# Windowed attention, Mish layer and experts on one core: the activation's intermediate moves into the low part's buffer, and two more weight pieces are converted during attention

## The chip, the cores and the metric

The kernel runs on one core of a Trainium2 chip. The metric is the device time of one execution in microseconds; the median of several executions counts. The program keeps five engines: TensorE (PE, matmuls; its weight loads are listed as PEld), VectorE (DVE), ScalarE (ACT), GpSimd (POOL) and SyncE (SP), which issues all DMA transfers here.

## The reference

What has to be computed, cut to the lines that matter (B 2, H 8, S 768, D 64; 1536 tokens, model width 512):

```python
# windowed attention: 4 sink columns and a window of 128
scores = np.where(keep, scale * q @ k.T, -1e9)
a = softmax(scores)
x = (a @ v)                                   # [1536, 512]
# Mish layer, weights in float64, d_ff 2048
h = x @ w_in
g = h * np.tanh(np.log1p(np.exp(np.minimum(h, 20.0))))
x = g @ w_out
# four experts of width 1024, weighted by domain probabilities
out += p[:, e:e + 1] * (np.maximum(x @ w1[e], 0.0) @ w2[e])
```

## The kernel before

All dense products are made from three fp32r matmuls: every operand is kept as a high part and a low part, and high times high, low times high and high times low are summed in PSUM (`TERMS`, L366). Activations have their parts in `xh` and `xl`; a layer's hidden tiles have theirs in `gh` and `gl`.

The dense work is cut into units of 512 hidden columns (`Experts.units`, L394). Units 0 to 3 are the Mish layer, units 4 to 11 the experts. A unit has its weights in four SBUF tiles, `wih`, `wil`, `woh` and `wol`; units take turns between two pools, `m_w0` and `m_w1` (L390, L597). A unit goes over the tokens in chunks. For each chunk `layer1` (L465) makes four hidden tiles: 12 matmuls into a PSUM tile `h` (L477), then the activation, which ends in `gh` and `gl`. `layer2` (L491) makes from these four output tiles `o` of 12 matmuls each (L504). `stream` (L449) writes the layer-1 steps of a chunk in between the layer-2 steps of the chunk before. Unit 0 has four chunks, called A, B, C and D here: tokens 0 to 255, 256 to 511, 512 to 1023 and 1024 to 1535. The four hidden tiles of chunk C are called C0 to C3 below; in the build of the kernel before they bear the names `h_1537`, `h_1636`, `h_1790` and `h_1941`.

The Mish activation (`mish`, L541) is a chain over two engines: four ACT operations from `h` to an exponential `r` (L549 to L552), one DVE operation (L553), one on ACT (L554), two on DVE (L555, L556; L556 is the last that reads `h`), one on ACT that writes `gh` and one on POOL that writes `gl` (L557, by way of L89 and L97).

While attention runs, the PSUM is shared with it: `x.psum(first, 1, 1)` (L575) gives unit 0 one bank for `h` (`m_pa`) and one for `o`, and `r` lies in an SBUF pool `m_pr` of one buffer. Chunks A and B and the tiles C0 to C3 use this one `h` bank. When attention has been written out, `first.close()` (L596) gives back its pools, `m_w1` takes their SBUF room, and new PSUM pools with three `h`, three `o` and two `r` banks are opened (L598); chunk D and all later work use these.

The Mish weights come as float64. `split_double` (L100) turns a piece of 128 x 1024 words into its two parts: one ACT operation (L116), seven on DVE (L117, L118, L119, L121, L122, L123, L124) and a DMA of the high part (L120). Units 0 and 1 and the first half of unit 2 are converted in the attention loop (L584 to L595): four pieces of unit 0 with the items 0 to 3, and six more, for unit 1 and for `wi` of unit 2, with the items named in `PARK`. These six are parked in DRAM by DMA (L120, L126) and loaded later by plain DMA (L434). The other pieces, `wo` of unit 2 and all of unit 3, are converted when their turn comes (L438).

The order of each engine's queue is not the order of the source: the framework's scheduler sorts the instructions of all engines when the program is built, and what comes out is fixed. Each engine then takes its queue in that order and waits at an instruction whose inputs or buffer are not ready.

Of the kernel before, what the change touches and what calls it, by code (L numbers as in the profile page):

```python
# [9 lines left out]
F32 = mybir.dt.float32  # L10
# [3 lines left out]
AF = mybir.ActivationFunctionType  # L14
ALU = mybir.AluOpType
PSUM = bass.MemoryType.PSUM

P = 128
BIG = 8.0e9
C2, C1, C0 = 0.4889076793633006, -0.9463237919407588, -0.8989585617169157  # L20
# [7 lines left out]
AHEAD = 2  # L28
LAG = 5
WARM = 12  # L30
PARK = (8, 10, 12, 14, 16, 18)

class Ctx:
    pass
# [42 lines left out]
def normalize_probs(c):  # L77
    nc = c.nc
    nc.vector.tensor_reduce(c.ps, c.pn, axis=mybir.AxisListType.X, op=ALU.add)
    nc.vector.tensor_scalar(c.ps, c.ps, 1e-9, None, ALU.add)  # L80
    nc.vector.reciprocal(c.ps, c.ps)
    nc.vector.tensor_tensor(c.pn, c.pn, c.ps.to_broadcast([P, 12, 4]), ALU.mult)
# [11 lines left out]
def split(c, hi, lo, src, eng_hi, eng_lo):  # L94

    copy(c, eng_hi, hi, src)
    eng_lo.tensor_tensor(lo, src, hi.bitcast(F32), ALU.subtract)  # L97
# [31 lines left out]
def load_item(c, b, hp, i, pool=None):  # L129

    w = c.KW[min(i, 1)]
    raw = c.stage.next() if pool is None else pool.tile([P, QW + c.KW[1]], F32, tag="qk", name="qk")
    off = c.OFF[i]
    c.nc.sync.dma_start(out=raw[:, 0:QW + w], in_=c.qk[b, hp, :, off:off + QW + w])
    return raw
# [29 lines left out]
def banded_masks(c):  # L165

    nc = c.nc
    rel, sink, diag, prev = c.parts
    m0, m1, m2 = c.masks
    nc.vector.tensor_scalar(sink, sink, c.ns, None, ALU.is_ge)  # L170
    nc.vector.scalar_tensor_tensor(diag, rel, c.win, diag, ALU.is_ge, ALU.add)
    nc.vector.scalar_tensor_tensor(m0[:, 0:P], diag, -BIG, sink, ALU.mult, ALU.mult)
    nc.vector.tensor_scalar(prev, rel, float(P), c.win, ALU.add, ALU.is_ge)
    nc.vector.scalar_tensor_tensor(m1[:, 0:P], prev, -BIG, sink, ALU.mult, ALU.mult)
    for m, at, x in ((m1, P, diag), (m2, 0, prev), (m2, P, sink[:, 0:SINKS]), (m2, SEG, diag)):
        nc.gpsimd.tensor_scalar(m[:, at:at + x.shape[1]], x, -BIG, 0.0, ALU.mult, ALU.add)
# [11 lines left out]
def attention_pools(c, ctx):  # L188
    nc = c.nc
    a = Ctx()  # L190
    a.qk = ctx.enter_context(c.tc.tile_pool(name="a_qk", bufs=4))
    v = c.acc[:, 8:12].rearrange("p a w -> p (a w)")
    a.v = Ring([v[:, 3 * P * n:3 * P * (n + 1)].rearrange("p (n d) -> p n d", n=3) for n in range(5)])
    a.p = ctx.enter_context(c.tc.tile_pool(name="a_p", bufs=3))
    a.st = v[0:4 * SINKS, 15 * P:16 * P]
    a.sm = ctx.enter_context(c.tc.tile_pool(name="a_sm", bufs=3))
    a.ps = ctx.enter_context(c.tc.tile_pool(name="a_ps", bufs=3, space=PSUM))
    a.tr = ctx.enter_context(c.tc.tile_pool(name="a_tr", bufs=2, space=PSUM))
    a.pv = ctx.enter_context(c.tc.tile_pool(name="a_pv", bufs=1, space=PSUM))
    a.vsk = c.vsk  # L200
    return a


def attention_values(c, a, b, hp, i):

    v = a.v.next()
    n0 = 0 if i else 1
    c.nc.sync.dma_start(
        out=v[:, n0:3],
        in_=c.v[b, hp, (2 * i - 1 + n0) * P:(2 * i + 2) * P, :].rearrange("(n p) d -> p n d", p=P),  # L210
    )
    return v
# [165 lines left out]
class Experts:  # L378
# [26 lines left out]

    def psum(self, ctx, nh, no, nr=0):
        tp = self.c.tc.tile_pool
        self.pr = ctx.enter_context(tp(name="m_pr", bufs=nr or 1, **(dict(space=PSUM) if nr else {})))
        self.pa = ctx.enter_context(tp(name="m_pa", bufs=nh, space=PSUM))
        self.pb = ctx.enter_context(tp(name="m_pb", bufs=no, space=PSUM))  # L410

# [129 lines left out]
    def mish(self, n, gh, gl, h):  # L541

        c, nc = self.c, self.c.nc
        cw = h.shape[-1]
        w, u = (self.tp.tile([P, self.CW], F32, tag=t, name=t)[:, 0:cw] for t in ("w", "u"))
        r = self.pr.tile([P, self.CW], F32, tag="r", name="r")[:, 0:cw]
        nc.scalar.activation(w, h, AF.Tanh, scale=0.5)  # L549
        nc.scalar.activation(w, w, AF.Square, scale=-0.5, bias=0.5)  # L550
        nc.scalar.activation(u, w, AF.Square, scale=C2, bias=C1)
        nc.scalar.activation(r, u, AF.Exp, bias=C0)  # L552
        nc.vector.scalar_tensor_tensor(u, w, 1.0, r, ALU.add, ALU.mult)  # L553
        nc.scalar.activation(u, u, AF.Square, scale=ROOT2, bias=-1.5 * ROOT2)  # L554
        nc.vector.scalar_tensor_tensor(u, u, 1.5, r, ALU.add, ALU.mult)  # L555
        nc.vector.scalar_tensor_tensor(w, u, 1.0, h, ALU.subtract, ALU.mult)  # L556
        split(c, gh, gl, w, nc.scalar, nc.gpsimd)  # L557


def run(gen, n=None):  # L560

    while n is None or n > 0:
        if next(gen, run) is run:
            return
        n = None if n is None else n - 1


def banded(c, ctx, raws):

    tc = c.tc  # L570
    banded_masks(c)
    first = ExitStack()
    x = Experts(c, ctx)
    w = x.weights(0)
    x.psum(first, 1, 1)  # L575
    a = attention_pools(c, first)
    steps = x.stream([(0, 0, QW), (0, QW, QW)] + [(0, t0, x.CW) for t0 in range(2 * QW, c.T, x.CW)] + later(c, x, 1))
    dram = ctx.enter_context(tc.tile_pool(name="park", bufs=1, space=bass.MemoryType.DRAM))
    w = chain(w, x.park(dram, 1, "wi"), x.park(dram, 1, "wo"), x.park(dram, 2, "wi"))
    items = c.items  # L580
    raws = dict(enumerate(raws))
    preps = {}
    done = 0
    for m, it in enumerate(items):  # L584
        while done <= min(m + AHEAD, len(items) - 1):
            raw = raws.pop(done) if done in raws else load_item(c, *items[done], pool=a.qk)
            preps[done] = raw, attention_values(c, a, *items[done])
            done += 1
        attention_item(c, a, *it, preps.pop(m))
        if m < 4 or m in PARK:  # L590
            run(w, 1)
        if m >= LAG:
            run(steps, 1)
        if m == 0:
            normalize_probs(c)  # L595
    first.close()  # L596
    x.wpool[1] = ctx.enter_context(tc.tile_pool(name="m_w1", bufs=1))  # L597
    x.psum(ctx, 3, 3, 2)  # L598
    run(x.weights(1))
    run(steps, 4 * (x.NF + 4) - 4 - (len(items) - LAG))  # L600
    rest(c, x, steps, 1)


def later(c, x, first):

    return [(n, t0, x.CW) for n in range(first, len(x.units)) for t0 in range(0, c.T, x.CW)]


def rest(c, x, steps, first):

    per = (c.T // x.CW) * (x.NF + 4)
    for n in range(first, len(x.units)):
        w = x.weights(n + 1) if n + 1 < len(x.units) else iter(())
        for _ in range(per // 2):
            run(steps, 2)
            run(w, 1)
        run(w)
    run(steps)
# [15 lines left out]
def swa_mish_experts_kernel(ctx: ExitStack, tc: tile.TileContext, qk, v, vsink, n_sink, window, w_in, w_out, probs, w1,  # L634
# [35 lines left out]
    with tc.If(flag > 0) as cmp:  # L670
        with ExitStack() as s:
            banded(c, s, raws)
# [69 lines left out]
```

## Time and profile before

| | us |
|---|---|
| median of 3 runs | 936.74 |
| lowest and highest of them | 935.36 and 939.33 |
| the profiled execution | 931.33 |
| its span, first to last instruction | 929.5 |
| PE busy in the span | 905.6 |
| DVE busy | 424.6 |
| ACT busy | 347.7 |
| POOL busy | 263.7 |

The span is what the trace covers; 1.8 us of the profiled execution lie outside it. Matmuls overlap in the array, so a busy PE isn't a PE at its best rate: at full clock 12 matmuls of 512 columns take 2.72 us from start to start, though one alone is shown with 0.39 us. A row of the timeline has start, duration, engine, line, operation, output and inputs, and in brackets the engine's idle time ahead of it with what ended it.

### The profile page before, as it was taken

What the parts mean: (1) busy time and instruction counts of PE and PEld (TensorE: products, weight loads), DVE (VectorE), ACT (ScalarE), POOL (GpSimd) and SP (SyncE); (2) the same over time, 40 slices, a digit from 0 to 9 for tenths busy, and PEclk for the clock granted to TensorE, in tenths of its full rate; (3) what the DMA queues carried; (4) which work ended last, traced back from release to release, by engine and by line L of the source; (5) the groups of instructions that cost most, each with busy time, mean ns of one, the idle gap of its engine ahead of it and who ended that gap; (6) DMA issues with size and microseconds to landing.
All of it is one profiled execution on the core that took longest, in us unless ns stands there. A gap on an engine that the chain in (4) does not pass through costs nothing.

```text
span 929.5 us, 11138 instructions
## 1 busy us (share of the span) xinstructions
PE 905.6 (97%) x4292; PEld 730.6 (79%) x4292; DVE 424.6 (46%) x770; ACT 347.7 (37%) x745; POOL 263.7 (28%) x217
## 2 busy tenths in 40 slices
PE   6999999799999999999999999999999999999997
PEld 4566767688888888888888888888888888888886
DVE  6999995247698555641112222222222222222222
ACT  4788875487767767722221111111111111111110
POOL 4586663122222434520220220221122112200000
PEclk8999999989999999999999999999999999999999
DMA  7757752062123011001110110110110010000012
GB/s 234 249 189 242 251 215 80 17 255 91 46 90 136 1 46 46 23 23 46 46 40 7 45 46 1 46 46 0 46 46 24 23 45 1 1 1 1 11 46 83
DMA packets 33790, 67.03 MB, mean 72 GB/s; under 512 B 4144, under 2 KB 12592, under 8 KB 33728
## 3 DMA queue, kind: packets, MB, share of 16 engines
q1 hardware_dynamic: 33728, 66.23, 21.1%
q8 instruction: 36, 0.59, 0.3%
q14 instruction: 26, 0.21, 0.1%
HBM read 51.54 MB, written 9.44 MB: 66 GB/s over the span
## 4 chain that ended last, share of the span: by engine, by line
PE 86%; DVE 10%; ACT 1%; DMA 1%; issue 0%; POOL 0%; DVEq 0%; ACTq 0%
PE h L477 42%; PE o L528 28%; PE o L504 14%; DVE pr L234 2%; DVE cv_h L119 1%; DVE cv_a L123 1%; PE pv L277 1%; DVE cv_a L117 1%; DVE cv_r L122 1%; DMA stage<-in_moe_w_in_dram 1%; PE sc L231 1%; PE tp L264 1%; DVE cv_a L121 1%; DVE xl L185 1%; DVE cv_a L118 0%
## 5 line engine op out<-in xcount | busy, mean ns | idle before, releaser
L477 PE MATMUL h<-xh,wih 128*128 128x512 f32 (+1 forms) x592 | 229.2, 387 | 0.3 <-DVE w L556 0.3
L477 PE MATMUL h<-xh,wil 128*128 128x512 f32 (+1 forms) x592 | 227.8, 385 | 0.0
L477 PE MATMUL h<-xl,wih 128*128 128x512 f32 (+1 forms) x592 | 226.8, 385 | 0.0
L486 ACT ACTIVATE gh<-h 128x512 fp32r<-128x512 f32 x96 | 57.4, 598 | 410.1 <-PE h L477 245.2
L487 DVE SCALAR_TENSOR_TENSOR gl<-h,gh 128x512 fp32r<-128x512 f32 x96 | 66.4, 691 | 208.1 <-ACT gh L486 207.9
L528 PE MATMUL o<-wol,gh 128*128 128x512 f32 (+1 forms) x388 | 150.1, 387 | 0.0
L528 PE MATMUL o<-woh,gh 128*128 128x512 f32 (+1 forms) x388 | 150.1, 387 | 0.0
L528 PE MATMUL o<-woh,gl 128*128 128x512 f32 (+1 forms) x388 | 149.9, 387 | 0.0
L536 DVE SCALAR_TENSOR_TENSOR acc<-o,pn,acc 128x512 f32<-128x512 f32 (+1 forms) x85 | 63.3, 745 | 176.2 <-PE o L528 176.2
L477 PEld LDWEIGHTS h<-xh,wih 128*128 128x128 f32 x592 | 111.8, 189 | 24.5 <-DVE cv_a L117 0.7
L477 PEld LDWEIGHTS h<-xl,wih 128*128 128x128 f32 x592 | 111.5, 189 | 22.6 <-issue 0.5
L477 PEld LDWEIGHTS h<-xh,wil 128*128 128x128 f32 x592 | 111.7, 189 | 22.3 <-DVE wil L124 0.3
L97 POOL TENSOR_TENSOR gl<-w,gh 128x512 fp32r<-128x512 f32 (+1 forms) x52 | 68.2, 1312 | 168.0 <-ACT gh L89 167.8
L504 PE MATMUL o<-gh,woh 128*128 128x512 f32 (+1 forms) x208 | 79.4, 382 | 5.4 <-ACT gh L89 5.4
L528 PEld LDWEIGHTS o<-wol,gh 128*128 128x128 f32 x388 | 72.9, 188 | 14.9
L528 PEld LDWEIGHTS o<-woh,gh 128*128 128x128 f32 x388 | 72.9, 188 | 14.9
L528 PEld LDWEIGHTS o<-woh,gl 128*128 128x128 f32 x388 | 72.8, 188 | 14.7
L504 PE MATMUL o<-gh,wol 128*128 128x512 f32 (+1 forms) x208 | 78.2, 376 | 0.0
L504 PE MATMUL o<-gl,woh 128*128 128x512 f32 (+1 forms) x208 | 77.4, 379 | 0.0
L87 POOL TENSOR_SCALAR wih<-stage 128x1024 fp32r<-128x1024 f32 x16 | 16.5, 1048 | 189.4 <-PE h L477 189.4
L553 DVE SCALAR_TENSOR_TENSOR u<-w,r 128x512 f32<-128x512 f32 (+1 forms) x52 | 34.4, 662 | 50.2 <-ACT r L552 49.9
L87 POOL TENSOR_SCALAR woh<-stage 128x1024 fp32r<-128x1024 f32 x16 | 16.5, 1048 | 141.0 <-PE o L528 122.2
(84 smaller groups left out, 1101.5 us busy)
## 6 DMA issues: line engine op xcount, KB each, us to landing
stage<-in_moe_w_dram SPq DMA_DIRECT2D x32, 512.0 KB, 3.7
stage<-in_moe_w_in_dram SPq DMA_DIRECT2D x8, 1024.0 KB, 6.6
stage<-in_moe_w_out_dram SPq DMA_DIRECT2D x8, 1024.0 KB, 5.0
qk<-in_qk_dram SPq DMA_DIRECT2D x16, 324.0 KB, 5.4
acc<-in_v_dram SPq DMA_DIRECT2D x16, 192.0 KB, 3.6
woh<-cv_h SPq DMA_DIRECT2D x6, 512.0 KB, 2.9
out_dram<-acc SPq DMA_DIRECT2D x11, 256.0 KB, 2.0
wih<-cv_h SPq DMA_DIRECT2D x4, 512.0 KB, 3.0
```

Source lines behind the costliest of these rows:

```text
L87: eng.tensor_scalar(out, src, 1.0, 0.0, ALU.mult, ALU.add)
L97: eng_lo.tensor_tensor(lo, src, hi.bitcast(F32), ALU.subtract)
L117: nc.vector.tensor_scalar(af, af, TINY_HI, HUGE_HI, ALU.max, ALU.min)
L119: nc.vector.scalar_tensor_tensor(h, w_hi, -0x40000000, a, ALU.bitwise_and, ALU.bitwise_or)
L234: nc.vector.tensor_tensor_reduce(out=o, in0=sc, in1=c.masks[t if i == 0 else 2][:, 0:sw], scale=-c.scale, scalar=3.0e38, op0=ALU.add, op1= ...
L477: nc.tensor.matmul(h, lhsT=wis[sw][:, k, fs], rhs=x[sx][:, k, cols], start=k == 0 and t == 0, stop=k == KT - 1 and t == 2,)
L486: nc.scalar.activation(gh, h, AF.Relu)
L487: nc.vector.scalar_tensor_tensor(gl, h, 0.0, gh.bitcast(F32), ALU.max, ALU.subtract)
L504: nc.tensor.matmul(o, lhsT=wos[sw][:, f, ds], rhs=g[f][sx], start=f == 0 and t == 0, stop=f == NF - 1 and t == 2,)
L528: nc.tensor.matmul(o, lhsT=g[f][sx][:, ds], rhs=wos[sw][:, f, ms], start=f == 0 and t == 0, stop=f == NF - 1 and t == 2,)
L536: nc.vector.scalar_tensor_tensor(y, o, pcol, y, ALU.mult, ALU.add)
L553: nc.vector.scalar_tensor_tensor(u, w, 1.0, r, ALU.add, ALU.mult)
```

## The change

Two things are done. In the attention phase `r` no longer has a pool: the exponential is written into the chunk's `gl` buffer, which the last operation of the chain overwrites with the low part, and the two DVE operations read it there. And `wo` of unit 2 joins the parked weights, with two more items, 20 and 22, in `PARK`.

```diff
-PARK = (8, 10, 12, 14, 16, 18)
+PARK = (8, 10, 12, 14, 16, 18, 20, 22)
@@ psum
-        self.pr = ctx.enter_context(tp(name="m_pr", bufs=nr or 1, **(dict(space=PSUM) if nr else {})))
+        self.pr = ctx.enter_context(tp(name="m_pr", bufs=nr, space=PSUM)) if nr else None
@@ mish
-        r = self.pr.tile([P, self.CW], F32, tag="r", name="r")[:, 0:cw]
+        rr, r = gl, gl.bitcast(F32)
+        if self.pr:
+            rr = r = self.pr.tile([P, self.CW], F32, tag="r", name="r")[:, 0:cw]
@@
-        nc.scalar.activation(r, u, AF.Exp, bias=C0)
+        nc.scalar.activation(rr, u, AF.Exp, bias=C0)
@@ banded
-    w = chain(w, x.park(dram, 1, "wi"), x.park(dram, 1, "wo"), x.park(dram, 2, "wi"))
+    w = chain(w, x.park(dram, 1, "wi"), x.park(dram, 1, "wo"), x.park(dram, 2, "wi"), x.park(dram, 2, "wo"))
```

The scheduler's order is the same in both builds for all engines up to the last operations of the attention phase, and differs from there. Lines from 545 on are 3 higher after the change. C0 to C3 are named `h_1526`, `h_1624`, `h_1794` and `h_1959` after it.

DVE, at the end of the attention phase, before the change: the rows behind the last attention score. `u`, `w` and `r` belong to the Mish chain, `xl` (from a PSUM tile `pv`) to an attention item's output, `cv_*` to a conversion.

```order
L123 SCALAR_TENSOR_TENSOR cv_a_2400<-stage_60,cv_a_2400 128x1024
L553 SCALAR_TENSOR_TENSOR u_1553<-w_1552,r_1554 128x512
L555 SCALAR_TENSOR_TENSOR u_1553<-u_1553,r_1554 128x512
L185 TENSOR_TENSOR xl_95<-pv_1863,xh_94 128x256
L556 SCALAR_TENSOR_TENSOR w_1552<-u_1553,h_1537 128x512
L185 TENSOR_TENSOR xl_95<-pv_1930,xh_94 128x256
L553 SCALAR_TENSOR_TENSOR u_1652<-w_1651,r_1653 128x512
L555 SCALAR_TENSOR_TENSOR u_1652<-u_1652,r_1653 128x512
L556 SCALAR_TENSOR_TENSOR w_1651<-u_1652,h_1636 128x512
```

The same place of DVE's queue after the change, from the second `xl` on; in the eleven rows ahead of it, between the first L123 and this `xl`, C0's chain is threaded with seven conversion rows in the same way.

```order
L185 TENSOR_TENSOR xl_95<-pv_1933,xh_94 128x256
L124 SCALAR_TENSOR_TENSOR cv_l_1945<-cv_a_1946,cv_r_1947 128x1024
L117 TENSOR_SCALAR cv_a_2842<-cv_a_2842 128x1024
L118 TENSOR_SCALAR cv_a_2842<-cv_a_2842 128x1024
L119 SCALAR_TENSOR_TENSOR cv_h_2844<-stage_60,cv_a_2842 128x1024
L556 SCALAR_TENSOR_TENSOR u_1640<-w_1639,gl_1638 128x512
L121 TENSOR_SCALAR cv_a_2842<-cv_h_2844 128x1024
L122 TENSOR_SCALAR cv_r_2843<-cv_h_2844 128x1024
L185 TENSOR_TENSOR xl_95<-pv_2028,xh_94 128x256
L123 SCALAR_TENSOR_TENSOR cv_a_2842<-stage_60,cv_a_2842 128x1024
L558 SCALAR_TENSOR_TENSOR u_1640<-u_1640,gl_1638 128x512
L559 SCALAR_TENSOR_TENSOR w_1639<-u_1640,h_1624 128x512
```

In all, 14 conversion rows now stand ahead of C1's last DVE operation: the L124 of the first piece of `wo` of unit 2, all seven of its second piece, and six of the first piece of unit 3, which had stood later.

PE, at the start of C2, before the change; `h_2083`, `h_2111` and `h_2153` are tiles of chunk D. Behind the 12 rows of C2 come 12 of `o_2069` (chunk B, 128x256).

```order
L477 MATMUL h_2111<-xh_94,wih_227 128x512
L477 MATMUL h_2111<-xh_94,wil_228 128x512
L477 MATMUL h_2153<-xh_94,wih_227 128x512
L477 MATMUL h_2153<-xh_94,wil_228 128x512
L477 MATMUL h_1790<-xh_94,wih_227 128x512
L477 MATMUL h_1790<-xh_94,wil_228 128x512
```

PE after the change, the same place: ahead of this piece stand the two matmuls with which the piece above ends its `h_2153` (here `h_2169`), the 12 of chunk B (here `o_2085`) and one of `h_2099`.

```order
L477 MATMUL h_2127<-xl_95,wih_224 128x512
L504 MATMUL o_2155<-gh_1539,woh_350 128x512
L504 MATMUL o_2155<-gh_1539,wol_351 128x512
L504 MATMUL o_2155<-gl_1540,woh_350 128x512
L477 MATMUL h_2169<-xl_95,wih_224 128x512
L504 MATMUL o_2197<-gh_1539,woh_350 128x512
L504 MATMUL o_2197<-gh_1539,wol_351 128x512
L504 MATMUL o_2197<-gl_1540,woh_350 128x512
L504 MATMUL o_2239<-gh_1539,woh_350 128x512
L504 MATMUL o_2239<-gh_1539,wol_351 128x512
L504 MATMUL o_2239<-gl_1540,woh_350 128x512
L477 MATMUL h_1794<-xh_94,wih_224 128x512
```

So 24 matmuls that stood behind C2 (12 of chunk B, three of chunk D, nine of chunk C's layer 2) stand ahead of it. Between C2 and C3 there were 12, three and 18 of these; now there are nine of layer 2.

SP, where unit 1's weights are loaded, after the change. Before it, one row `L372 DMA stage_60<-in_moe_w_in_dram` stood directly ahead of the first L434 row.

```order
L120 DMA wo2h_1777<-cv_h_1783 128x1024
L372 DMA stage_60<-in_moe_w_in_dram 128x2x1024
L126 DMA wo2l_1778<-cv_l_1780 128x1024
L120 DMA wo2h_1777<-cv_h_1948 128x1024
L372 DMA stage_60<-in_moe_w_in_dram 128x2x1024
L126 DMA wo2l_1778<-cv_l_1945 128x1024
L434 DMA wih_2073<-wi1h_786 128x1024
L434 DMA wil_2074<-wi1l_787 128x1024
```

The six rows ahead of the L434 are one load that was there, one that came earlier and the four parking transfers. In the list of waits, the first L434 row waited for DVE, PE and POOL before the change, and for PE, ACT and POOL after it.

## Rows read from the trace of the kernel before

**Rows 1.** The profile page's first part: busy time and share of span.
```profile
span 929.5 us, 11138 instructions
PE 905.6 (97%) x4292; PEld 730.6 (79%) x4292; DVE 424.6 (46%) x770; ACT 347.7 (37%) x745; POOL 263.7 (28%) x217
```

**Rows 2.** Stretches: length, busy time and count by engine, granted clock, DMA share.
```profile
147.00:200.00 53.00, 47.65 (x241) 38.21 (x238) 16.13 (x25) 30.09 (x58) 8.82 (x7) 0.94 0.35 127
200.00:929.50 729.50, 724.59 (x3209) 600.28 (x3207) 271.51 (x376) 207.25 (x347) 160.75 (x102) 1.00 0.11 38
147.66:163.53 15.87, 15.87 (x103) 12.57 (x102) 4.71 (x8) 7.37 (x17) 1.28 (x1) 1.00 0.20 67
```

**Rows 3.** Waits: who waited for whom, total us, times, longest.
```profile
PE o L504 <- ACT gh L89: 5.4, 1, 5.4
```

**Rows 4.** Waits of SP's DMA queue.
```profile
SPq L434 <- DVE u L555: 35.2, 1, 35.2
```

**Rows 5.** Timeline of PE from C2 to behind its longest pause.
```profile
165.51 0.39 PE L477 MATMUL h<-xh,wih 128*128 128x512 f32 x1
...
168.23 0.28 PE L504 MATMUL o<-gh,woh 128*128 128x256 f32 x1
...
169.66 0.63 PE L477 MATMUL h<-xl,wih 128*128 128x512 f32 x2
...
171.73 0.39 PE L504 MATMUL o<-gh,woh 128*128 128x512 f32 x1
...
174.45 0.44 PE L477 MATMUL h<-xh,wih 128*128 128x512 f32 x1
...
177.23 0.39 PE L504 MATMUL o<-gh,woh 128*128 128x512 f32 x1
...
184.78 0.79 PE L504 MATMUL o<-gh,woh 128*128 128x512 f32 x1 [5.35 <-ACT gh L89]
185.37 0.63 PE L504 MATMUL o<-gh,wol 128*128 128x512 f32 x1
185.80 0.63 PE L504 MATMUL o<-gh,woh 128*128 128x512 f32 x1
...
190.92 0.43 PE L477 MATMUL h<-xl,wih 128*128 128x512 f32 x1
```

**Rows 6.** Timeline of DVE, the Mish chains of C1 and C2.
```profile
158.50 0.42 DVE L185 TENSOR_TENSOR xl<-pv,xh 128x256 fp32r<-128x256 f32 x1 [7.93 <-ACT xh L184]
...
162.84 0.69 DVE L556 SCALAR_TENSOR_TENSOR w<-u,h 128x512 f32<-128x512 f32 x1
...
173.65 0.69 DVE L556 SCALAR_TENSOR_TENSOR w<-u,h 128x512 f32<-128x512 f32 x1
```

**Rows 7.** Timeline of ACT, in the chain of C2.
```profile
169.12 0.63 ACT L550 ACTIVATE w<-w 128x512 f32<-128x512 f32 x1
169.86 0.38 ACT L510 ACTIVATE acc<-o 128x256 f32<-128x256 f32 x1
170.14 0.62 ACT L551 ACTIVATE u<-w 128x512 f32<-128x512 f32 x1
```

**Rows 8.** Stretches again, only instructions on tile cv_a: DVE, ACT, clock, DMA.
```profile
216.00:300.00 84.00, 34.67 (x31) 5.68 (x5) 1.00 0.28 101
```

**Rows 9.** The same stretch, only line L122: DVE, clock, DMA.
```profile
216.00:300.00 84.00, 3.41 (x5) 1.00 0.28 101
```

**Rows 10.** Stretches as in Rows 2: earlier pauses of PE and what follows them.
```profile
14.00:17.00 3.00, 0.00 (x0) 0.00 (x0) 0.83 (x4) 0.70 (x1) 1.65 (x2) 0.98 1.00 324
17.00:23.00 6.00, 5.54 (x19) 2.83 (x19) 5.55 (x17) 4.12 (x15) 2.51 (x3) 0.50 0.94 372
30.20:31.10 0.90, 0.00 (x0) 0.00 (x0) 0.90 (x5) 0.00 (x0) 0.90 (x1) 1.00 0.05 12
31.10:35.00 3.90, 3.38 (x20) 2.03 (x20) 3.90 (x13) 3.13 (x11) 0.24 (x2) 1.00 0.82 271
```

## The prediction

> **What bounds the kernel now.** I read the page's totals first: PE is busy for 905.6 of 929.5 us [rows 1]. Then a few long stretches: from 200 us on, PE is busy for 724.59 of 729.50 us at full clock [rows 2], and in the timeline its 512-column matmuls follow each other there at the best rate. What can be won or lost lies ahead of 200 us, in the attention phase and the passage from it to unit 1. Both builds have the same order on every engine up to about 147.6 us, so only the passage is left: 147 to 200 us, with 47.65 us of PE at a clock of 0.94 [rows 2].
>
> In the passage the longest wait of PE is 5.35 us ahead of 184.78, and what ends it is ACT's `gh` [rows 3, 5], no transfer. That `gh` is C3's. C0 to C3 share one `h` bank, so C3's matmuls can't start before DVE's L556 has read C2's `h`, C2's not before C1's is read, and so on: matmuls, Mish chain, matmuls, Mish chain. PE fills the chain's time with work of chunks B and D and of chunk C's layer 2. C3 starts at 174.45, 0.11 us behind the end of C2's L556 at 174.34 [rows 5, 6]; there the fill was just enough. Behind C3 it isn't, and PE stands for 5.35 us.
>
> **The change part by part.**
>
> The exponential in `gl`: the same operations on the same engines in the same place of their queues, so nothing is added; the order shows no new wait on the exponential's row in any of the eight tiles of chunks A and B. Between 0 and 147 us I count 0.
>
> The weights of unit 1: their load on SP waits 35.2 us for a DVE operation, L555 [rows 4], the last reader of `r` in its SBUF pool. This wait goes. What is late next for that load is the last attention item (PE, ACT, POOL in its list of waits) and, on SP's queue, the parking transfers put ahead of it, the last of which needs the second piece's L124. I put that at 160 to 164 us in place of 183.42. But nobody waits for these weights before: unit 1's first matmul stands, in both builds, 39 matmuls and more behind the one that stood 5.35 us, and PE takes its matmuls in order. The gain is 0.
>
> The pieces that leave the time behind 200 us: two of `wo` of unit 2 and most of one of unit 3, each 7 DVE operations with a mean of (34.67 + 3.41) / 36 = 1.06 us, 7.4 us a piece [rows 8, 9]. PE has no pause there that they cause [rows 2], so taking them away gives 0; PE's own work is the cover. Two MB more of plain loads replace them where DMA has a share of 0.11.
>
> The same pieces in the passage: 14 operations ahead of the end of C1's chain, 14 x 1.06 = 14.8 us. DVE was busy for 4.71 of the 15.87 us between 147.66 and 163.53 [rows 2], so 11.16 us were free (7.93 of them in one wait [rows 6]) and 3.7 us are not covered. C1's last DVE operation ended at 163.53 (162.84 + 0.69 [rows 6]) and now ends at 167.2 at the earliest. Twice DVE must also wait for an ACT conversion operation, 1.14 us each (5.68 / 5 [rows 8]), which itself waits for DVE: 169.5 at the latest.
>
> That wait isn't what sets PE, by the new order. 24 matmuls that stood behind C2 now run ahead of it: 12 of 256 columns, 169.66 - 168.23 = 1.43 us [rows 5], and 12 of 512 columns, which take 174.45 - 171.73 = 2.72 us [rows 5]. Everything else ahead of C2 is the same set. C2 starts at 165.51 + 4.15 = 169.66 [rows 5], 0.2 to 2.5 us later than DVE has freed the bank. The late chain of C1 is covered by these matmuls; without them it would cost its 3.7 us itself.
>
> What was moved ahead of C2 is missing behind it. From C2's start to C3's start there were 8.94 us [rows 5]. The chain between them is unchanged but for one ACT operation: the evacuation L510 of chunk B, which pushed L551 from 169.75 to 170.14 [rows 7], now comes ahead of the chain. So 8.94 - 0.39 = 8.55 us, and C3 starts at 178.21, **3.76 us later**. PE has work for 2.72 us (C2) and 9 x 0.227 = 2.04 us of that, until 174.42, then a **new pause of 3.8 us**.
>
> From C3's start to the end of the old pause nothing changes in order: 184.78 - 174.45 = 10.33 us [rows 5], all in the chain C3's matmuls, tanh, ..., `gh`. PE goes on at 188.54 where it went on at 184.78, with the same set of matmuls done. Behind this the queues hold the same work, and PE had no further pause; so 3.76 us arrive at the end in full.
>
> The clock. After the pause of 3 us at 14 us the granted clock was 0.50, that is 1.2 GHz, from 17 to 23 us; after one of 0.9 us at 30.2 it stayed at 1.00 [rows 10]. The new pause of 3.8 us is nearest to the first. C3's 12 matmuls stand in the chain right behind it; at the lower level they start every 0.43 us (185.37, 185.80 [rows 5]) and not every 0.227: 12 x 0.2 = 2.4 us if all of them are hit, 0 if none. I take **1.4 us**, since the drop needn't come at once or last for all twelve. The slow stretch from 184.78 to 190.92 [rows 5] stays behind the old pause; it cost 14 x 0.2 = 2.8 us and may be up to 1 us more or less.
>
> Here a rule weighs against my term. The Trainium skill, "TensorE: Matmul & The Clock Gate", section "What's actually happening", holds that the time lost while the clock comes up again varies from run to run and is so small a part of a usual kernel that one shouldn't fit it when modelling. By that the clock term would be 0 and the sum the first rival's below. The trace has a number against leaving it out, the six slow microseconds from 17 to 23 us [rows 10].
>
> Sum: 3.76 + 1.4 = **5.2 us**. The profiled execution (931.33, of which 929.5 are its span) would become 936.5; the median shown, 936.74, lies 5.4 us above that execution, and with it I forecast **941.9**.
>
> **The rivals.**
>
> First, the chain as above, but C3's matmuls keep the full clock: 3.8 us, 940.5. For it speaks the pause at 30.2 us, against it the one at 14 us.
>
> Second, nothing is lost: the new order is only a swap, because DVE frees C2's bank and C2's chain runs while PE has other work, so that C3 starts when PE gets there. That needs PE's fill behind C2 to be 3.8 us longer than the 2.04 us that the order shows, or a C2 chain that is 3.8 us shorter than its 8.5. If it were so, 936.7 to 938. That the conversions don't reach the passage at all (the change not doing what it says) falls in here, and the order speaks against it.
>
> Third, faster: unit 1's weights, there 20 us earlier, let its first matmuls fill the old pause. That would give back up to 5.35 us and the 2.8 us of slow clock behind it: 936.74 - 8.1 = 928.6. It decides at the order: those matmuls would have to stand ahead of the one that waits for C3's `gh`. They don't. The Trainium skill, "Perfetto Trace Analysis", section "Optimization Strategy", says that gaps which keep coming back on the engine that should be full can mean that SBUF or PSUM lacks room for the next tile. By it the 35.2 us for `r`'s room would be the fault and this rival the outcome; PE's pause is ended by ACT, though, and the room that lacks is the one `h` bank, which the change leaves as it is.
>
> Fourth, slower still: C1's chain ends later than 169.66, and C2 waits for DVE. Each microsecond beyond costs one. POOL's work beside DVE is the likeliest cause; 2 us of it give 943.9.
>
> **How the numbers follow.** The forecast with a clock term (940.9 to 943) has 0.45, the first rival 0.27, the fourth 0.12, the second 0.11, the third 0.05. The likeliest is the forecast, 941.9. A measurement of this kernel can tell about 0.5%, 4.7 us, from no change. Slower by more than that are the fourth and most of the forecast: 0.12 + 0.40 = 0.52, and 0.02 of the first rival: 0.54. Within 0.5%: 0.05 + 0.25 + 0.11 = 0.41. Faster: 0.05. The range leaves out the third rival, a part of the second and the far end of the fourth: 937.8 to 944.6.
>
> **What would show it.** In the profile after: the DVE stretch from 150 to 158 us full of L117 to L124; unit 1's L434 transfers near 162 us; a pause of PE of 3 to 4 us ahead of C3's first matmul, ended by DVE's L559, and after it a second pause of about 5 us, still ended by `gh`; C3 starting near 178 us; the granted clock down at C3 or not, which decides between 940.5 and 941.9. I would be wrong if PE has no pause ahead of C3, if unit 1's matmuls fill the pause, or if PE pauses behind 200 us.

## The result, and the profile after

The changed kernel takes 942.31 us (median of 9 runs, 937.82 to 944.11), the kernel before 936.65 us (9 runs, 931.10 to 939.33); the ratio is 1.0057, with a 95% interval of 1.0030 to 1.0085. The forecast was 941.9 us in a range of 937.8 to 944.6. The profiled execution took 942.14 us, 940.3 of which are its span.

The totals of the page, as [rows 1], and the two long stretches, as [rows 2] (length, busy time and count of PE, PEld, DVE, ACT, POOL, then granted clock, DMA share, GB/s):

```profile
span 940.3 us, 11148 instructions
PE 915.0 (97%) x4292; PEld 737.2 (78%) x4292; DVE 426.6 (45%) x770; ACT 349.0 (37%) x745; POOL 263.8 (28%) x217
```

```profile
147.00:200.00 53.00, 44.49 (x226) 35.33 (x226) 30.58 (x39) 26.23 (x51) 11.67 (x9) 0.91 0.51 181
200.00:940.30 740.30, 735.26 (x3254) 609.25 (x3253) 263.94 (x369) 216.19 (x364) 163.68 (x104) 1.00 0.12 38
```

Behind 200 us PE is again without a pause, at full clock. C0 starts 6.06 us later in this trace than in the one before, so its stretch from 147 to 200 us stands beside this one of the kernel before:

```profile
140.94:193.94 53.00, 47.65 (x245) 38.12 (x245) 20.29 (x29) 29.57 (x60) 11.27 (x10) 0.94 0.24 83
```

DVE is busy for 30.58 us where it was for 20.29, and PE for 44.49 where it was for 47.65. The waits of PE from 140 to 200 us, as [rows 3], show one more:

```profile
PE o L504 <- ACT gh L89: 4.9, 1, 4.9
PE h L477 <- DVE w L559: 3.6, 1, 3.6
```

The timeline of PE from C0 to the end of the passage, as [rows 5] (start, duration, engine, line, operation, output and inputs, in brackets the idle time and what ended it). C0 starts at 147.15, C2 at 175.35, C3 at 183.88:

```profile
147.15 0.50 PE L477 MATMUL h<-xh,wih 128*128 128x512 f32 x1
...
175.35 0.39 PE L477 MATMUL h<-xh,wih 128*128 128x512 f32 x1
...
179.43 0.84 PE L504 MATMUL o<-gl,woh 128*128 128x512 f32 x3
183.88 0.79 PE L477 MATMUL h<-xh,wih 128*128 128x512 f32 x1 [3.60 <-DVE w L559]
184.47 0.63 PE L477 MATMUL h<-xh,wil 128*128 128x512 f32 x1
...
188.74 0.63 PE L477 MATMUL h<-xl,wih 128*128 128x512 f32 x1
...
190.01 0.44 PE L504 MATMUL o<-gh,woh 128*128 128x512 f32 x1
...
196.75 0.66 PE L504 MATMUL o<-gh,woh 128*128 128x512 f32 x1 [4.91 <-ACT gh L89]
```

There is a pause of 3.60 us ahead of C3, all 12 matmuls of C3 behind it start some 0.43 us apart (0.79 us long the first, 0.63 the others), and then comes the old pause. DVE in the same passage, as [rows 6]: the last conversion operation, and the last operations of C1's and C2's chains:

```profile
170.94 1.22 DVE L123 SCALAR_TENSOR_TENSOR cv_a<-stage,cv_a 128x1024 f32<-128x1024 uint32 x1
172.07 0.68 DVE L558 SCALAR_TENSOR_TENSOR u<-u,gl 128x512 f32<-128x512 f32 x1
172.86 0.69 DVE L559 SCALAR_TENSOR_TENSOR w<-u,h 128x512 f32<-128x512 f32 x1
...
183.13 0.69 DVE L559 SCALAR_TENSOR_TENSOR w<-u,h 128x512 f32<-128x512 f32 x1
```

C1's chain ends at 173.55, 1.8 us before PE gets to C2; C2's ends at 183.82, and 0.06 us later C3 starts.

The two profiled executions are 10.8 us apart, about twice the difference of the medians. Where it arose is seen from the landmarks of PE. The start of C0 in the kernel before:

```profile
141.09 0.50 PE L477 MATMUL h<-xh,wih 128*128 128x512 f32 x1
```

The table has the landmarks for four traces; the first and the second half alone are experiments below, each with the order of one of the two kernels.

| us | before | first half alone | both halves | second half alone |
|---|---|---|---|---|
| start of C0 | 141.09 | 147.95 | 147.15 | 144.93 |
| C0 to C2 | 24.42 | 26.28 | 28.20 | 28.66 |
| C2 to C3 | 8.94 | 8.94 | 8.53 | 8.51 |
| C3 to the end of the old pause | 10.33 | 10.37 | 12.87 | 11.73 |
| from there to the end of the span | 744.72 | 743.16 | 743.55 | 744.07 |
| C0 to the end of the span | 788.41 | 788.75 | 793.15 | 792.97 |

Up to C0 all four have the same instruction order on PE, DVE and ACT, and yet C0 starts up to 6.9 us apart; 6.06 of the 10.8 us lie there and are not the change's (the last section has what they are). From C0 on, the change costs 793.15 - 788.41 = 4.7 us in this pair. One row needs a word: from C0 to C2 the first half alone has the order of the kernel before and takes 1.86 us longer. Its granted clock was 0.81 from 147 to 160 us, and 1.00 in the three other traces, so 24.42 is the length to compare with.

### The profile page after: what moved, and what is told of

It reads as the page before. It is cut to its first block, busy times and chain, and to the rows that moved or that the text cites. A ratio compares the mean times of both kernels' runs of the same rounds, so it can differ in the third digit from the quotient of the medians.

```text
span 940.3 us, 11148 instructions
## 1 busy us (share of the span) xinstructions
PE 915.0 (97%) x4292; PEld 737.2 (78%) x4292; DVE 426.6 (45%) x770; ACT 349.0 (37%) x745; POOL 263.8 (28%) x217
## 4 chain that ended last, share of the span: by engine, by line
PE 88%; DVE 8%; ACT 1%; DMA 1%; issue 0%; DVEq 0%; ACTq 0%
PE h L477 42%; PE o L528 28%; PE o L504 13%; PE sc L231 2%; DVE pr L234 2%; PE pv L277 2%; PE tp L264 1%; DVE cv_h L119 1%; DVE cv_a L123 1%; DMA stage<-in_moe_w_in_dram 1%; DVE cv_r L122 1%; DVE cv_a L117 1%; PE pv L283 1%; DVE u L556 0%; DVE xl L185 0%; DVE cv_a L121 0%
## 5 line engine op out<-in xcount | busy, mean ns | idle before, releaser
L97 POOL TENSOR_TENSOR gl<-w,gh 128x512 fp32r<-128x512 f32 (+1 forms) x52 | 67.2, 1294 | 171.3 <-ACT gh L89 161.6
L504 PE MATMUL o<-gh,woh 128*128 128x512 f32 (+1 forms) x208 | 79.9, 384 | 4.9 <-ACT gh L89 4.9
L504 PE MATMUL o<-gh,wol 128*128 128x512 f32 (+1 forms) x208 | 78.6, 378 | 0.0
L504 PE MATMUL o<-gl,woh 128*128 128x512 f32 (+1 forms) x208 | 77.3, 378 | 0.2 <-POOL gl L97 0.2
L238 ACT ACTIVATE pr<-pr,mx 128x260 f32<-128x260 f32 (+2 forms) x96 | 46.5, 486 | 22.8 <-DVE mx L234 21.7
```

The source lines that it names most:

```text
L238: nc.scalar.activation(o, o, AF.Exp, bias=mx[:, e:e + 1], scale=-1.0, accum_out=sm[:, e:e + 1])
L504: nc.tensor.matmul(o, lhsT=wos[sw][:, f, ds], rhs=g[f][sx], start=f == 0 and t == 0, stop=f == NF - 1 and t == 2,)
```

## Experiments

Each ratio compares a run's times with those of the kernel before taken along with it; it need not be the quotient of two medians shown.

**The two halves apart.** The first half alone: `r` in `gl`, the six pieces of before. Its order is that of the kernel before on every engine.

```diff
-        r = self.pr.tile([P, self.CW], F32, tag="r", name="r")[:, 0:cw]
+        rr, r = gl, gl.bitcast(F32)
+        if self.pr:
+            rr = r = self.pr.tile([P, self.CW], F32, tag="r", name="r")[:, 0:cw]
...
-        nc.scalar.activation(r, u, AF.Exp, bias=C0)
+        nc.scalar.activation(rr, u, AF.Exp, bias=C0)
```

> The kernel before with only the first half of the change: r in gl, no SBUF pool for r, six parked pieces as before. Every engine has the instruction order of the kernel before. My theory (the loss is all in the passage and comes from the two more pieces): no difference, 936.7, ratio 1.000 within 0.003; C2 to C3 about 8.9 us apart, no pause ahead of C3, the old pause of 5.3 us ahead of the L504 that waits for gh; SP's first L434 no longer waits for DVE but is issued some 20 us earlier. First rival (the exponential's new place costs something in chunks A and B, or its longer hold on gl): slower by 1 to 5 us. Second rival (the earlier weights fill the pause): 928.6.

Measured: 936.52 us (12 runs), ratio 1.0004 (0.9980 to 1.0029). Two lines of its trace, the wait of PE in the passage and SP's first loads of unit 1's weights (shortest, median and longest in ns, then the first and the last start in us):

```profile
PE o L504 <- ACT gh L89: 5.4, 1, 5.4
L434 SPq DMA_DIRECT2D wih<-wi1h x2: 339/384/430, 171.7 to 172.5; - x2
```

The load is issued at 171.7 us and PE goes on at 193.54: the weights are there some 20 us before anybody reads them, and the pause is what it was. The 35.2 us of [rows 4] were a wait that nobody waited for.

The second half alone: eight pieces, `r` in its SBUF pool. PE, DVE and ACT have the changed kernel's order; SP's load of unit 1's weights still waits for DVE's L555, as in [rows 4], here for 21.5 us.

```diff
-PARK = (8, 10, 12, 14, 16, 18)
+PARK = (8, 10, 12, 14, 16, 18, 20, 22)
...
-    w = chain(w, x.park(dram, 1, "wi"), x.park(dram, 1, "wo"), x.park(dram, 2, "wi"))
+    w = chain(w, x.park(dram, 1, "wi"), x.park(dram, 1, "wo"), x.park(dram, 2, "wi"), x.park(dram, 2, "wo"))
```

> The kernel before with only the second half: two more parked pieces, items 20 and 22, r in its SBUF pool as before. PE, DVE and ACT have the order of the changed kernel. My theory: the whole loss, 941 to 943, ratio 1.004 to 1.007; a pause of 3.4 to 3.8 us ahead of C3 ended by DVE's last Mish operation, then the pause ended by gh. Rival (the loss needs both halves, or is the place of r): the time of the kernel before, 936.7.

Measured: 941.29 us (12 runs), ratio 1.0059 (1.0034 to 1.0084): the whole loss. PE's timeline at C3:

```profile
182.10 0.80 PE L477 MATMUL h<-xh,wih 128*128 128x512 f32 x1 [3.60 <-DVE w L556]
182.70 0.63 PE L477 MATMUL h<-xh,wil 128*128 128x512 f32 x1
...
184.83 0.47 PE L477 MATMUL h<-xh,wih 128*128 128x512 f32 x1
185.14 0.40 PE L477 MATMUL h<-xh,wil 128*128 128x512 f32 x1
...
193.83 0.80 PE L504 MATMUL o<-gh,woh 128*128 128x512 f32 x1 [5.35 <-ACT gh L89]
```

The new pause is the same to a hundredth; of C3's 12 matmuls six are slow here, twelve in the changed kernel.

**The shared bank.** If C2 and C3 wait only because C0 to C3 share a bank, giving them banks of their own must take the pauses away. The steps of the dense work are written one per attention item; when only the first 15 are written inside the attention loop, C2 and C3 are allocated behind `x.psum(ctx, 3, 3, 2)`.

```diff
-        if m >= LAG:
+        if LAG <= m < LAG + 15:
             run(steps, 1)
...
-    run(steps, 4 * (x.NF + 4) - 4 - (len(items) - LAG))
+    run(steps, 4 * (x.NF + 4) - 4 - 15)
```

> The kernel before, with only 15 of the steps of the dense work written inside the attention loop in place of 19, so that C2 and C3 are allocated behind the switch of the PSUM pools and get two of the three new h banks; nothing else is changed, the scheduler sorts anew. My theory (the shared h bank makes PE stand): C2 and C3 no longer wait for the activation of the tile before, both pauses of the passage go, and with the 5.35 us go the 2.8 us of slow clock behind it: 928 to 930, ratio 0.991 to 0.993. Rival (the bank isn't the limit, the Mish chain's own length or its two buffers for w and u are): pauses of the same size at another place, 935 to 938.

Measured: 929.93 us (9 runs), ratio 0.9935 (0.9905 to 0.9965), faster than both kernels. All waits of PE between 130 and 250 us:

```profile
PE sc L231 <- DVE mx L234: 0.7, 1, 0.7
PE h L477 <- ACT xh L184: 0.7, 2, 0.5
PE h L477 <- DVE w L556: 0.3, 1, 0.3
```

Both the 5.35 us and the slow matmuls behind them are gone; the granted clock is 1.00 from 147 to 210 us. The last score matmul, here and in the kernel before:

```profile
142.25 0.93 PE L231 MATMUL sc<-qk 64*128 64x260 f32 x2 [0.72 <-DVE mx L234]
```

```profile
136.10 1.01 PE L231 MATMUL sc<-qk 64*128 64x260 f32 x2 [0.72 <-DVE mx L234]
```

Up to it PE has the same matmuls in the same order in both. From it to the end of the span the trace has 928.4 - 142.25 = 786.2 us, against 929.5 - 136.10 = 793.4 before: 7.2 us less, of the 8.1 (5.35 and 2.8) that the pause and its slow stretch were put at.

The edit also gives C2 and C3 `r` and `o` tiles of the new pools. That the bank of `h` made PE stand is told by what ended the pause ahead of C3: DVE's L559, the last operation that reads C2's `h`. With `r` in `gl`, in the changed kernel, that pause is there all the same.

The same edit on the changed kernel:

> The changed kernel with the same edit: 15 steps inside the loop, C2 and C3 in the new h banks; eight parked pieces, r in gl while the first pools are open. My theory: without the serial bank the conversions in the passage lie beside PE's other work and cost nothing, so the time is that of the same edit on the kernel before, 928 to 931. Rival (DVE's 14 conversion operations delay the Mish chains themselves, whatever the banks): 3 to 5 us slower than the same edit on the kernel before, 932 to 935.

Measured: 932.12 us (12 runs), ratio 0.9959 (0.9934 to 0.9984). The changed kernel gains 9 to 10 us by it (942.31 to 932.12; ratio 1.0057 to 0.9959). The time lies 1 us above the theory's 928 to 931, and the 2 us to the same edit on the kernel before are less than the rival's 3 to 5; as the intervals of the two runs overlap, they are not certain. The traces have a cause for most of it (930.5 - 142.63 = 787.9 us from the last score matmul on, 1.7 more). A wait of PE, and DVE's timeline there:

```profile
PE o L504 <- DVE xl L185: 1.3, 1, 1.3
```

```profile
170.96 1.22 DVE L123 SCALAR_TENSOR_TENSOR cv_a<-stage,cv_a 128x1024 f32<-128x1024 uint32 x1
172.10 0.42 DVE L185 TENSOR_TENSOR xl<-pv,xh 128x256 fp32r<-128x256 f32 x1
```

An `xl`, the output of an attention item, stands behind a conversion in DVE's queue, and PE waits for it until 172.57. It is the one wait of PE from 130 to 250 us that the same edit on the kernel before doesn't have, so beside PE's work the conversions cost 1.3 us here: neither theory had this place.

With 17 steps in the loop, in the changed kernel, C3 alone gets a new bank:

> The changed kernel with 17 steps inside the loop: C3 alone is allocated behind the switch of the pools and gets a new h bank, C2 keeps the old one; the scheduler sorts anew. My theory (the new pause is C3 waiting for C2's Mish chain in the same bank): no pause ahead of C3, and as C3 comes earlier the pause that waits for its gh goes too or shrinks: 931 to 935, ratio 0.995 to 1.000. Rival (what makes PE stand is the Mish chain's lateness by the conversions): a pause of 3 us or more stays, 938 to 942.

Measured: 936.16 us (12 runs), ratio 0.9992 (0.9967 to 1.0018), 6 us less than the changed kernel. Its longest waits of PE behind 10 us:

```profile
PE o L504 <- ACT gh L89: 5.4, 1, 5.4
PE sc L231 <- DMA qk<-in_qk_dram: 3.4, 1, 3.4
```

The pause ahead of C3 is gone, though the 14 conversion operations are still where they were. The old pause stays at full size; it now waits for C2's `gh`, as C2 is the last tile in the old bank. That it would go or shrink was wrong, and so the time came out above the 931 to 935 expected.

Two more ways to get banks. With 13 steps in the loop, C1 to C3 in new banks:

> The kernel before with 13 steps inside the loop: C1, C2 and C3 behind the switch of the pools. If the bank is all there was to gain in the passage: the time of the run with C2 and C3 there, 0.9935, within 0.003. Rival (more can be filled, C1's wait for the scores' banks costs nothing): 1 to 2 us faster than that, ratio 0.991 to 0.993; or slower, where C1 has to wait for the banks of the scores and chunk C's layer 2 comes late, ratio 0.996 to 1.000.

Measured: 932.95 us (12 runs), ratio 0.9983 (0.9964 to 1.0003). The ratio lies in the range of the second rival, 0.996 to 1.000, not at the 0.9935 of the run with C2 and C3. Yet the passage gains as much: PE has no pause of more than 1.0 us in it, the granted clock is 1.00 from 140 to 210 us, and from the last score matmul to the end of the span the trace has 926.3 - 140.56 = 785.7 us, 0.4 less than that run. But this execution, 928.11, is the fastest of the 12. PE's order differs from that of the kernel before from 109 us on, in the attention phase, and whether the others lose the rest there or it is chance isn't decided.

Two `h` banks during attention and two score banks (`x.psum(first, 2, 1)`, `a_ps` with `bufs=2`):

> The kernel before with the PSUM split otherwise in the attention phase: two h banks in place of one, two score banks in place of three; the scheduler sorts anew. My theory: the serial chain of C0 to C3 is broken, no pause in the passage, and attention, which DVE sets, loses little: 929 to 933, ratio 0.993 to 0.998. Rival (the third score bank is needed): attention is 5 us or more longer, which eats the gain: ratio 1.000 to 1.005.

Measured: 943.09 us (6 runs), ratio 1.0077 (1.0055 to 1.0099). That is above both expectations. The pauses of the passage are gone, but the last score matmul starts at 173.37 us, with 889 matmuls ahead of it where the kernel before has 788, and PE is busy for 919.2 us in place of 905.6 [rows 1]. So with a bank taken from the scores, and the order that comes with it, more is lost than the pauses cost; what makes PE's work longer was not followed up.

**The clock by itself.** Four runs had matmuls whose result nobody reads, to keep PE busy in a pause. In the old pause, on the kernel before:

```diff
+            if n == 0 and t0 == 2 * QW:
+                self.gc = g
...
     x.psum(ctx, 3, 3, 2)
+    for f, count in ((2, 20),):
+        d = x.pr.tile([P, x.CW], F32, tag="r", name="d")
+        for _ in range(count):
+            c.nc.tensor.matmul(d, lhsT=x.w[0][1][0][:, f, 0:P], rhs=x.gc[f][0], start=True, stop=True)
```

> The kernel before with 20 more matmuls of 512 columns whose result nobody reads: they read the hidden tile C2, write to a bank of the new pools, and stand in PE's queue where PE waits 5.35 us for C3's gh, between the layer-2 matmuls of C2 and those of C3. No dependence of the real work changes. They take 20 x 0.227 = 4.5 us of the pause. Theory of the clock term (the pause is what lowers the granted clock): the clock stays at 1.00 behind it, and the 2.8 us of the slow matmuls behind the pause come back: ratio 0.997, 932 to 934 where the kernel before has 935 to 937. Rival (the clock goes down for another reason, or the rule that it needn't be modelled): ratio 1.000.

Measured: 940.02 us (12 runs), ratio 1.0048 (1.0020 to 1.0077). PE's timeline (L506 and L558 are the L504 and L556 of the kernel before):

```profile
191.88 6.40 PE L604 MATMUL d<-gh,woh 128*128 128x512 f32 x20 [4.78 <-DVE w L558]
198.12 0.39 PE L506 MATMUL o<-gh,woh 128*128 128x512 f32 x1
```

They did not fill the pause. They waited for DVE's last operation of C3's chain, the last that reads the old `h` bank, so it seems that their bank of the new pools lies on that one. They ran behind the pause, for 6.24 us. That is 1.7 us more than 20 x 0.227, and the first real matmul after them is at full rate: these matmuls took the slow stretch on themselves. What an unbroken PE would do to the clock here this run doesn't say.

In the pause at 14 us [rows 10], 26 matmuls of 256 columns, on the kernel before and on the one with 15 steps:

```diff
+    if (b, hp, i) == (0, 0, 0):
+        d = c.xp.pa.tile([P, 512], F32, tag="h", name="d")
+        for _ in range(26):
+            nc.tensor.matmul(d[:, 0:256], lhsT=c.ident, rhs=pr[:, 0, 1, 0:256], start=True, stop=True)
...
+    c.xp = x
```

> The kernel before with 26 more matmuls of 256 columns whose result nobody reads, at the first transposes of the attention phase, so that they fill the pause of 3 us at 14 us in which PE waits for a DMA. Theory (the time to C0's first matmul, 141.1 to 148.0 us in four traces with one and the same order, differs by how long the granted clock stays at 0.50 behind this pause): the clock stays at 1.00, C0 starts at 139 to 142 us, and the time is 931 to 933, ratio 0.994 to 0.997, with less spread. Rival (DVE sets the attention phase, or the clock falls at another pause): C0 at 145 to 148 us, ratio 1.000 to 1.003.

> Both gains together, on the kernel before: C2 and C3 in the new h banks (15 steps in the loop) and the 26 matmuls nobody reads in the pause at 14 us. If the two are independent the time is the sum: 6 us from the banks and 3 to 6 us from the clock, 924 to 927, ratio 0.988 to 0.991. Rival (the early fill gives nothing): the time of the banks alone, 929 to 931.

Measured: 955.21 us, ratio 1.0202 (1.0162 to 1.0243), and 947.86 us, ratio 1.0122 (1.0079 to 1.0166), 6 runs each. The price was mis-sized: in the trace each of these matmuls shows as two and takes 0.44 us, 11.4 us in all, for a pause of 3. Eight of them:

> The early fill again with 8 matmuls nobody reads in place of 26: in the run with 26 each showed as two records and took 0.44 us, 11.4 us in all, far more than the pause of 3 us; 8 take 3.5 us. Theory: the clock stays at 1.00 behind 14 us, the last score matmul comes at 134 to 137 us as in the profiled run of the kernel before and not at 140.7 to 142.4, ratio 0.994 to 0.998. Rival (the matmuls put off real transposes by as much as they give): ratio 1.000 to 1.004.

Measured: 943.50 us (6 runs), ratio 1.0093 (1.0064 to 1.0122), above both expectations. The stretches of its trace around the place, and two rows of PE's timeline:

```profile
17.00:24.00 7.00, 4.76 (x24) 2.50 (x23) 6.37 (x11) 2.72 (x9) 0.00 (x0) 1.00 0.78 288
25.00:48.00 23.00, 23.00 (x81) 13.08 (x82) 14.95 (x51) 13.35 (x43) 7.16 (x13) 0.50 0.60 209
```

```profile
22.94 0.83 PE L231 MATMUL sc<-qk 64*128 64x128 f32 x4 [1.61 <-DVE mx L234]
24.60 0.49 PE L481 MATMUL h<-xh,wih 128*128 128x256 f32 x1 [0.83 <-ACT xh L184]
```

With the pause filled, the clock is 1.00 where it had been 0.50 in the kernel before, from 17 us on; but it falls at 25 us, behind two shorter pauses of 1.61 and 0.83 us, and stays down until 48. The early fill isn't a remedy: the slow stretch moved and grew, and the last score matmul came at 145.35 us, not at the 134 to 137 expected.

## Why the prediction was right, point by point

**Where the time goes.** That only the passage matters held: the first half has a ratio of 1.0004, the second the whole loss, and PE has no pause behind 200 us.

**C2 later by 4.15 us**, because 24 matmuls stand ahead of it: 28.20 - 24.42 = 3.78 in the changed kernel, 28.66 - 24.42 = 4.24 in the second half alone. That PE's order sets this and not DVE was right too: C1's chain ended 1.8 us before C2 started, inside the 0.2 to 2.5 forecast. On the clock of the trace before that is 167.5 us, at the lower end of 167.2 to 169.5. The fourth rival's cause was there in small: while POOL's L97 ran (161.19 to 163.93), one L124 took 1.98 us where the one before it took 1.23. It didn't reach C2.

**C2 to C3 in 8.55 us**: 8.53 and 8.51. The missing L510 was the 0.4 us.

**A new pause of 3.8 us ahead of C3, ended by L559**: 3.60 in both traces, ended by that operation. The sum of these three, C3 later by 3.76, came out as 3.37 and 3.81.

**The clock term of 1.4 us, between 0 and 2.4.** From C3's start to the end of the old pause there are 10.33 and 10.37 us with the old order, 12.87 and 11.73 with the new: 2.5 and 1.4 us more, twelve and six slow matmuls. The first lies just above the upper bound, the second on the value taken; that the forecast of 1.4 met one of them to a tenth is luck. The first rival, that C3 keeps its clock, happened in neither trace. The slow stretch behind the old pause varies by itself: from that pause to the end the four traces have 743.2 to 744.7 us, and the longest and the shortest both have the old order. The rule of the Trainium skill that stood against this term ("TensorE: Matmul & The Clock Gate", "What's actually happening") says that the loss while the clock comes up varies from run to run and is too small a share of a usual kernel to be fitted. The traces agree with both statements: twelve and six slow matmuls behind the same pause, 2.5 us at most, 0.3% of the time. But that was up to half of the effect asked for, and leaving it out would have given the first rival's 940.5.

**The old pause unchanged**: 4.91 and 5.35 us for 5.35. Right; in the first, two of the nine matmuls between C3 and the pause were still slow (189.16 to 190.01) and took 0.4 us of it.

**The earlier weights give nothing**: loads at 168.3 us in the changed kernel, which is 162.2 on the clock of the trace before (C0 is 6.06 us later), in the 160 to 164 forecast. The third rival fell with the first half alone. The Trainium skill's "Perfetto Trace Analysis", "Optimization Strategy", which was weighed as the rule behind that rival, says that a gap which keeps coming on the engine to be kept full can mean too little SBUF or PSUM for the next tile. The trace agrees with it in the PSUM part: the missing room was the `h` bank, and giving C2 and C3 new ones took 7.2 us out of the trace. It was not the room of `r`, the longer wait by far.

**The sum**: 5.2 us forecast; 4.2 to 4.7 from C0 on, each of the two traces with the new order against each with the old; 5.7 between the medians. The parts of the changed kernel against the kernel before are 3.37 (C3 later) and 2.54 (slow matmuls), less 1.17 behind the old pause, where fewer matmuls were slow: 4.74. So part of the agreement is that a slow stretch longer than forecast at C3 and a shorter one behind the old pause nearly cancel; the prediction allowed each its range, but did not forecast that. **What was not foreseen** is that the profiled executions differ by another 6.06 us ahead of C0. The median shown was used as the base, 5.4 us above the profiled execution, and so the forecast didn't suffer; had the two traces been compared as they are, the loss would have been put at about twice its size.

## What to carry to other kernels

Ask of a long wait who waits for the waiter: SP's 35.2 us cost nothing, while the chain through one shared bank, with just enough matmuls between two links, cost what was moved out from between them. Work that is moved ahead of a link isn't free because PE is busy all the while: count what is left behind it. When two traces are compared, set them side by side at a landmark ahead of the change; here more than half of their difference lay before it.

## What the runs showed of the hardware

The kernel before spreads from 929.5 to 939.6 us by itself, and the time goes with the granted clock: of its 72 runs taken along with the experiments, the 20 fastest (up to 932.3 us) have a mean clock of 0.984 to 0.989, the 20 slowest (from 937.5 us on) one of 0.975 to 0.980. The traces show where the clock was low. The stretch from 17 to 45 us, in the kernel before and in the changed one; the order in it is the same:

```profile
17.00:45.00 28.00, 25.78 (x137) 14.94 (x137) 27.04 (x75) 21.19 (x68) 14.23 (x16) 0.88 0.77 271
```

```profile
17.00:45.00 28.00, 27.47 (x110) 15.44 (x111) 23.87 (x65) 18.49 (x59) 11.39 (x13) 0.65 0.73 254
17.00:36.00 19.00, 18.64 (x61) 10.37 (x63) 16.50 (x43) 10.65 (x33) 5.93 (x6) 0.50 0.73 264
```

Behind PE's wait for one and the same load, which ends at 17 us (3.17 us long in the first, 1.85 in the second), the granted clock stayed at 0.50, the level of 1.2 GHz, from 17 to 23 us in the first execution and from 17 to 36 us in the second; with the first half alone the mean from 17 to 45 us is 0.66, with the second 0.63. PE is busy nearly all of the time and gets 110 records done where it got 137. Later stretches differ too. From 0 to 140 us, in the kernel before, with the second half alone, in the changed kernel and with the first half alone:

```profile
0.00:140.00 140.00, 126.40 (x805) 86.46 (x807) 130.00 (x363) 105.64 (x328) 88.90 (x104) 0.95 0.69 231
0.00:140.00 140.00, 127.63 (x788) 86.00 (x788) 126.01 (x348) 101.87 (x318) 85.67 (x101) 0.93 0.67 223
0.00:140.00 140.00, 129.00 (x782) 88.53 (x782) 125.21 (x346) 100.99 (x315) 83.54 (x100) 0.90 0.67 223
0.00:140.00 140.00, 127.86 (x781) 87.71 (x781) 124.70 (x346) 101.20 (x315) 83.04 (x100) 0.90 0.67 223
```

The mean clock falls from 0.95 over 0.93 to 0.90 and 0.90, and C0 starts at 141.09, 144.93, 147.15 and 147.95 us, in the same order. No run set the clock by itself without other changes, so that the clock makes the spread is read from these rows and not tested. Why the clock comes back after 6 us once and after 19 in another execution, no run here tells.
